# Grouped-query decode attention with a Mish MLP on one core: the first query weights in one load ahead of the first keys, two weight matrices in long rows with their operands turned on the chip, and the residual loaded mid-run

## The chip, the cores and the metric

One core of one Trainium2 chip. The metric is the device time of one execution in microseconds; the median of three runs of the kernel before is 1331.87 us (1331.69 to 1333.33).

## The reference

```python
# B=8 tokens, D=512, 32 query heads over 8 key/value heads, 8192 keys, head size 128, F=1792
xn = layernorm(x)                                    # no scale, no shift
q  = (xn @ wq) -> 8 x 32 heads x 128                 # wq [512, 4096]
s  = q . k_cache * 128**-0.5                         # 4 query heads share one key/value head
o  = softmax(s) . v_cache                            # k_cache, v_cache [8, 8, 8192, 128] fp32
A  = o @ wo                                          # wo [4096, 512]
h  = xn @ w1 + b1                                    # w1 [512, 1792]
m  = h * tanh(softplus(h)) @ w2                      # w2 [1792, 512]
out = x + A + m
```

All is fp32. Keys and values are 268 MB each, and the four weight matrices together 24 MB: nearly all of the work is reading 561 MB once.

## The kernel before

The work is cut into 32 units, `j = 8 * m + b`: one token `b` and one pair `m` of key/value heads (so 8 query heads). A unit needs one load of 8 MiB of keys and one of 8 MiB of values; each is one DMA that gives every partition one row of 64 KiB (`load_unit`, L127).

**Places.** One tile `kv` holds everything that streams: 160 KiB a partition. Values always land at `V_AT` (the first 64 KiB). Keys of even and odd units land at `K_AT[0]` and `K_AT[1]`, which start at 64 KiB and 96 KiB and overlap by half. Only the keys of unit 0 land at `V_AT`. So the values of unit 0 can be loaded only when the scores of unit 0 have read their keys to the end; the keys of unit j+1 when the first half of the scores of unit j is through; the values of unit j when `values(j-1)` has read the ones before. `w1` lands inside the place of the even keys (`W1_AT`), and the Mish layer computes there too, so the keys of unit 2 wait for the Mish layer. The four pieces of `wo` land at `V_AT` after the last unit, `w2` at `W2_AT`.

**Order.** The schedule is written by hand: every engine takes its instructions in the order of the code, and all large loads go through SP's one DMA queue in that order. A load is issued when SP reaches it and what occupies its place has been read.

**A unit** (the loop at L483): 32 score matmuls in two halves, with the load of the next keys issued between the halves (`scores`, L308); the row maximum on VectorE, turned over TensorE, and the exponential on ScalarE (`softmax`, L326); 32 matmuls of the unit before with its values, summed on VectorE (`values`, L374); then the issue of this unit's values; the masked query weights of the next unit (`key_weights`, L294, VectorE); the turning of the exponentials (`turn`, L352: 4 matmuls, 4 transposes and 2 long reductions on VectorE); and `merge` (L393), which puts the finished heads of the unit before into `oT`. In unit 0 the Mish layer (`mish`, L399) stands between. Once per pair of heads the query weights are loaded into `ws` (`load_q`), multiplied (`project`, L245) and spread over the partitions (`spread`, L277).

**The head of the program.** `x` comes over ACT's queue; VectorE normalizes it (L188 to L201) after it has built several selection matrices out of an identity that GpSimd makes. `wq` of the first pair is cut in two: 384 rows as three rows of 4 KiB per partition (`q0_3`, 1.5 MiB, SP's queue, ahead of the first keys), and the last 128 rows as 32 partitions with 16 KiB each (`q0_x`), in four DMAs that GpSimd issues, alternating with four DMAs for the bias `b1`. `q0_x` lies where the keys of unit 1 land. `project(0)` needs both parts, and two transposed copies of x for them (`xn3`, `xnx`).

**The tail.** After the last unit, `outputs` (L451) multiplies each of four pieces of `wo` with `oT`, `down` (L463) multiplies the three pieces of `w2` with the Mish result, and the residual, which was put into `xres` at the start by four matmuls (L225), is added (L550).

Of the kernel before, what the change touches and what calls it, by code (L numbers as in the profile page):

```python
# [53 lines left out]

D3 = 3
XQ = slice(64, 96)
XAT = ROW + ROW // 2


# [8 lines left out]
LOAD_Q, MAKE_Q, SPREAD_Q = 4, 5, 7  # L68


@with_exitstack
def kernel(
# [37 lines left out]
    gsel = const.tile([B, B, B], F32, name="gsel")  # L110
    xn4 = const.tile([P, CC, B], F32, name="xn4")
    xnT = const.tile([P, CC, B], F32, name="xnT")
    xn3 = const.tile([P, D3, B], F32, name="xn3")
    xnx = const.tile([P, CC, B], F32, name="xnx")
    qr = const.tile([P, DI, H2 * B], F32, name="qr")
    xres = const.tile([P, P], F32, name="xres")
    oT = const.tile([P, NP, H2, B], F32, name="oT")
# [24 lines left out]
    q0 = wq[:CC].rearrange("j p f -> (j p) f")  # L142
    q0_3 = ws[:, : D3 * BW]
    q0_x = kv[XQ, XAT : XAT + CC * BW]
    for r in range(4):
        n = FG // 8
        nc.gpsimd.dma_start(  # L147
            b1_sb[:, n * r : n * (r + 1)], b1.rearrange("(g c f) -> c g f", g=B, c=4)[r]
        )
        nc.gpsimd.dma_start(  # L150
            q0_x[r::4], q0[D3 * P :].rearrange("(e r i) f -> r e (i f)", r=4, i=CC)[r]
        )
    nc.sync.dma_start(q0_3, q0[: D3 * P].rearrange("(p i) f -> p (i f)", i=D3))
    k_t = {0: load_unit(kT, 0, V_AT)}
    w1_t = kv[:, W1_AT : W1_AT + 7168].rearrange("p (j f) -> p j f", j=2 * CC)
# [20 lines left out]
    for d in range(2):  # L176
        nc.vector.reduce_sum(
            rsel[:, d * REP : (d + 1) * REP],
            ident.rearrange("p (c d k h) -> p d h c k", c=2, d=2, h=REP)[:, d],
            axis=AX.XY,  # L180
        )
    nc.vector.tensor_copy(
        gsel, ident[:B, :B].rearrange("p (g o) -> p g o", o=1).to_broadcast([B, B, B])
# [20 lines left out]
    for c in range(CC):  # L204
        nc.tensor.transpose(
            M[:, 32 + c * B : 32 + (c + 1) * B], xc[:, c * P : (c + 1) * P], ident[:B, :B]
        )
    for c in range(D3):
        nc.tensor.transpose(
            M[:, 64 + c * B : 64 + (c + 1) * B], xc[:, c : D3 * P : D3], ident[:B, :B]  # L210
        )
    for c in range(CC):
        nc.tensor.matmul(
            M[XQ, 96 + c * B : 96 + (c + 1) * B],
            xc[:, D3 * P + c :: CC],
            ident[:B, :B],
            start=True,
            stop=True,
        )
    nc.vector.tensor_copy(xn3.rearrange("p c b -> p (c b)"), M[:, 64 : 64 + D3 * B])  # L220
    nc.vector.tensor_copy(xnx[XQ].rearrange("p c b -> p (c b)"), M[XQ, 96:128])
    nc.vector.tensor_copy(xn4.rearrange("p c b -> p (c b)"), M[:, 0:32])
    nc.vector.tensor_copy(xnT.rearrange("p c b -> p (c b)"), M[:, 32:64])
    for g in range(G):
        nc.tensor.matmul(  # L225
            M[Q * g : Q * g + B, 256:384],
            ident[:B, :B],
            x_sb[:, g * P : (g + 1) * P],
            start=True,
            stop=True,  # L230
        )
    nc.vector.tensor_copy(xres, M[:, 256:384])
# [12 lines left out]
    def project(m):  # L245

        w = ws.rearrange("p (c f) -> p c f", c=CC)
        terms = [(c, xn4[:, c, :], w[:, c]) for c in range(CC)]
        if m == 0:
            wx = q0_x.rearrange("p (c f) -> p c f", c=CC)  # L250
            terms = [(c, xn3[:, c, :], w[:, c]) for c in range(D3)]
            terms += [((c + D3) % CC, xnx[XQ, c, :], wx[:, c]) for c in range(CC)]
        for d in range(2):
            for n, (c, xt, wt) in enumerate(terms):
                nc.tensor.matmul(  # L255
                    H[Q * c : Q * c + B, :],
                    xt,
                    wt[:, d * 512 : (d + 1) * 512],
                    start=(n < CC),
                    stop=(n >= len(terms) - CC),  # L260
                )
# [12 lines left out]
        nc.vector.tensor_scalar_mul(qT, M[:, 192 : 192 + H2 * B], DH**-0.5)  # L274
        return qT
# [117 lines left out]
    def merge(j, os):  # L393
        m, b = divmod(j, B)
        nc.tensor.matmul(M[:, 168 : 168 + H2], os, hsel, start=True, stop=True)  # L395
        nc.vector.tensor_mul(oT[:, m, :, b], M[:, 168 : 168 + H2], RT.pop(j))


    def mish(w1_t, b1_sb, flat):  # L399
        hp = H[:, :FG]  # L400
        for c in range(CC):
            for g in range(G):
                nc.tensor.matmul(  # L403
                    hp[Q * g : Q * g + B, :],
                    xnT[:, c, :],
                    w1_t[:, c * 2 + g // 2, g % 2 * FG : (g % 2 + 1) * FG],
                    start=(c == 0),
                    stop=False,
                )
        for g in range(G):  # L410
            for e in range(2):
                nc.tensor.matmul(
                    hp[Q * g : Q * g + B, e * (FG // 2) : (e + 1) * (FG // 2)],
                    gsel[:, 2 * g + e, :],
                    b1_sb,
                    start=False,
                    stop=(e == 1),
                )
# [27 lines left out]
        nc.vector.tensor_copy(aT, turned.rearrange("p (j q) -> p j q", q=Q)[:, :, :B])  # L446
# [3 lines left out]

    def outputs(m, t):  # L451
        w = t.rearrange("p (u f) -> p u f", u=4)
        for d in range(2):
            for h in range(REP):
                nc.tensor.matmul(
                    A[Q * h : Q * h + B, :],
                    oT[:, m, d * REP + h, :],
                    w[:, d * 2 + h // 2, h % 2 * D : (h % 2 + 1) * D],
                    start=(m == 0 and d == 0),
                    stop=(m == NP - 1 and d == 1),  # L460
                )
# [14 lines left out]
    nc.sync.dma_start(w1_t, w1.rearrange("j p f -> p j f"))  # L476
# [3 lines left out]
    key_weights(0)  # L480

    v_t = {}
    for j in range(UNITS):  # L483
# [15 lines left out]
        if j + 1 < UNITS:  # L499
# [3 lines left out]
            key_weights(j + 1)  # L503
        if j == 0:
            mish(w1_t, b1_sb, kv[:, W1_AT : W1_AT + 6 * FG])
# [5 lines left out]
        if j > 0:  # L511
            merge(j - 1, os)
        if more and b == SPREAD_Q - 1:
# [20 lines left out]
    merge(UNITS - 1, os)  # L534
    outputs(NP - 1, w_o[NP - 1])
# [54 lines left out]
```

## Time and profile before

| | |
|---|---|
| median of 3 runs | 1331.87 us |
| the profiled execution, first to last instruction (its span) | 1330.5 us |
| DMA bytes | 561.79 MB, mean 422 GB/s |
| PE busy (matmul) | 984.8 us, 74% |
| VectorE busy | 516.0 us, 39% |
| ScalarE, GpSimd busy | 40.2 us, 6.4 us |
| share of the chain that ended last: DMA, PE | 73%, 22% |
| mean granted TensorE clock | 0.885 |

The page gives the profiled execution no time but its span; it is 1.4 us under the median of the runs. Times in the trace are microseconds from the first instruction. The rows used below are of six kinds: the page's 40 slices of the span (how busy the DMA engines were and what they moved), a table by stretches (`A:B`, then per engine its busy time and instructions in brackets, then the granted clock, the share of time in which the 16 DMA engines were busy, and GB/s), the chain of work that ended last (start, length, what), the timeline of one engine (start, length, engine, line, operation), who waited for whom, and the DMA issues with the median time to landing. "SPq" is the sequencer that issues SP's DMAs.

### The profile page before, as it was taken

What the parts mean: (1) busy time and instruction counts of PE and PEld (TensorE: products, weight loads), DVE (VectorE), ACT (ScalarE), POOL (GpSimd) and SP (SyncE); (2) the same over time, 40 slices, a digit from 0 to 9 for tenths busy, and PEclk for the clock granted to TensorE, in tenths of its full rate; (3) what the DMA queues carried; (4) which work ended last, traced back from release to release, by engine and by line L of the source; (5) the groups of instructions that cost most, each with busy time, mean ns of one, the idle gap of its engine ahead of it and who ended that gap; (6) DMA issues with size and microseconds to landing.
All of it is one profiled execution on the core that took longest, in us unless ns stands there. A gap on an engine that the chain in (4) does not pass through costs nothing.

```text
span 1330.5 us, 11234 instructions
## 1 busy us (share of the span) xinstructions
PE 984.8 (74%) x5071; PEld 338.3 (25%) x5071; DVE 516.0 (39%) x730; ACT 40.2 (3%) x88; POOL 6.4 (0%) x17
## 2 busy tenths in 40 slices
PE   1888776877867976776887777687786787677766
PEld 0422222222322222222322222222232222222222
DVE  2065444134443234444244444413444332444431
ACT  1000000000000000000000000000000000000000
POOL 1000000000000000000000000000000000000000
PEclk9999789988889888879988888998897998888898
DMA  9889999999999999999999999999999999999997
GB/s 341 338 346 432 420 438 436 436 428 436 428 436 434 434 432 428 427 439 438 426 432 432 438 430 434 426 438 434 430 430 434 432 434 436 428 428 434 430 415 321
DMA packets 13839, 561.79 MB, mean 422 GB/s; under 512 B 1464, under 2 KB 1592, under 8 KB 4800
## 3 DMA queue, kind: packets, MB, share of 16 engines
q1 hardware_dynamic: 13520, 560.53, 98.2%
q8 instruction: 39, 0.64, 0.2%
q0 software_dynamic: 256, 0.53, 0.1%
q10 hardware_dynamic: 16, 0.02, 0.0%
q14 instruction: 8, 0.07, 0.0%
HBM read 561.01 MB, written 0.07 MB: 422 GB/s over the span
## 4 chain that ended last, share of the span: by engine, by line
DMA 73%; PE 22%; DVE 2%; SPq 2%; issue 0%; POOL 0%; ACT 0%; DVEq 0%; POOLq 0%
DMA kv<-in_v 70%; PE o L378 19%; DMA kv<-in_wq 2%; DMA kv<-in_w 2%; SPq L528 2%; PE s L316 1%; DVE pt L366 1%; PE x L281 1%; PE h L255 0%; PE m L266 0%; PE h L403 0%; DVE kv L434 0%; DVE tr L360 0%; POOL kv L147 0%; DVE wk L299 0%
## 5 line engine op out<-in xcount | busy, mean ns | idle before, releaser
L316 PE MATMUL s<-kv,wk 128*64 128x512 f32 x2048 | 505.7, 657 | 180.7 <-DMA kv<-in_kT 178.1
L378 PE MATMUL o<-kv,pt 128*32 128x512 f32 x2048 | 262.3, 671 | 51.8 <-DMA kv<-in_v 42.2
L316 PEld LDWEIGHTS s<-kv,wk 128*64 128x64 f32 x2048 | 156.0, 152 | 505.0 <-issue 321.5
L366 DVE TENSOR_REDUCE pt<-tr 64x512 f32<-64x2048 f32 x64 | 241.3, 3771 | 1.6
L328 DVE TENSOR_REDUCE nm<-s 128x1 f32<-128x512 f32 x32 | 22.1, 692 | 374.2 <-PE s L316 374.1
L355 PE MATMUL x<-e,perm 128*128 128x512 f32 x256 | 126.4, 639 | 2.0 <-ACT qr L288 2.0
L378 PEld LDWEIGHTS o<-kv,pt 128*32 128x32 f32 x2048 | 68.4, 122 | 219.3 <-issue 164.9
L386 DVE TENSOR_SCALAR os<-o,isel 128x128 f32<-128x128 f32 x32 | 11.2, 351 | 265.4 <-PE o L378 265.4
L360 DVE STREAM_TRANSPOSE tr<-x 128x512 f32<-128x512 f32 x128 | 78.6, 671 | 0.0
L299 DVE TENSOR_TENSOR wk<-qr,mask 128x512 f32<-128x512 f32 x64 | 63.0, 1026 | 19.8 <-ACT qr L288 19.8
L355 PEld LDWEIGHTS x<-e,perm 128*128 128x128 f32 x256 | 48.9, 201 | 74.6 <-issue 72.2
L347 ACT ACTIVATE e<-s,nmx 128x512 f32<-128x512 f32 x32 | 22.0, 688 | 1092.8 <-DVE nmx L344 1092.8
L388 DVE SCALAR_TENSOR_TENSOR os<-o,isel,os 128x128 f32<-128x128 f32 x96 | 33.7, 351 | 3.4
L329 PE MATMUL m<-ident,nm 128*1 128x128 f32 x32 | 8.7, 273 | 30.1 <-DVE nm L328 30.1
L340 PE MATMUL m<-ident,nx 1*128 1x1 f32 x32 | 7.0, 219 | 24.2 <-DVE nx L336 24.2
L281 PE MATMUL x<-qT,tr 128*128 128x64 f32 x128 | 19.3, 315 | 3.0 <-ACT qr L288 2.7
L358 DVE RECIPROCAL rt<-m 128x8 f32<-128x8 f32 x32 | 6.6, 208 | 34.0 <-PE m L356 34.0
L281 PEld LDWEIGHTS x<-qT,tr 128*128 128x128 f32 x128 | 18.1, 226 | 6.2 <-ACT qr L288 3.3
L395 PE MATMUL m<-hsel,os 128*128 128x8 f32 x64 | 12.4, 266 | 9.3 <-DVE rt L358 9.3
L349 DVE TENSOR_SCALAR lsel<-rsel,l 128x8 f32<-128x8 f32 x32 | 7.4, 231 | 30.1 <-ACT e L347 30.1
L329 PEld LDWEIGHTS m<-ident,nm 128*1 128x1 f32 x32 | 2.5, 79 | 58.3 <-DVE nm L328 58.3
L356 PEld LDWEIGHTS m<-lsel,ones 128*128 128x128 f32 x64 | 12.2, 190 | 15.6 <-issue 15.3
(98 smaller groups left out, 172.2 us busy)
## 6 DMA issues: line engine op xcount, KB each, us to landing
kv<-in_wo SPq DMA_DIRECT2D x4, 2048.0 KB, 25.9
ws<-in_wq SPq DMA_DIRECT2D x3, 2048.0 KB, 35.2
kv<-in_w SPq DMA_DIRECT2D x1, 3584.0 KB, 24.7
kv<-in_w SPq DMA_DIRECT2D x1, 2048.0 KB, 37.0
ws<-in_wq SPq DMA_DIRECT2D x1, 1536.0 KB, 7.6
kv<-in_w SPq DMA_DIRECT2D x1, 1024.0 KB, 20.7
kv<-in_kT SPq DMA_DIRECT2D x32, 29.5
kv<-in_wq POOLq DMA_DIRECT2D x4, 128.0 KB, 25.1
```

Of the source, the lines that this page charges most:

```text
L281: nc.tensor.matmul(X[:, half, k * 64 : (k + 1) * 64], wide[:, half * 8 + k], qT, start=True, stop=True,)
L299: nc.vector.tensor_mul(w[:, :, d], q[:, :, d].to_broadcast([P, DI, NH * G, REP]), mask[:, d * NH * G : (d + 1) * NH * G] .rearrange("p (o ...
L316: nc.tensor.matmul(S[64 * c : 64 * (c + 1), :], w[:, i].rearrange("p d k h -> p (d k h)"), kk[:, i, c, :], start=(part == 0 and n == 0), s ...
L328: nc.vector.tensor_reduce(nm, S, axis=AX.X, op=ALU.max, negate=True)
L347: nc.scalar.activation(e, S, AF.Exp, bias=nmx, accum_out=l)
L355: nc.tensor.matmul(X[:, g], perm[:, g], e, start=True, stop=True)
L360: nc.vector.transpose(tr.rearrange("p (l t) c -> p t l c", t=TL)[:, tl], X.rearrange("p g (t q l) -> p t l g q", t=TL, q=PP)[:, tl],)
L366: nc.vector.tensor_reduce(pt8[half, :, :, d * REP : (d + 1) * REP].rearrange("p c y h -> p y c h"), tr[half].rearrange("p y (g c h) -> p y ...
L378: nc.tensor.matmul(O[Q * q : Q * (q + 1), :], pt8[:, c, TL * l : TL * (l + 1), :].rearrange("p t h -> p (t h)"), vt[:, 512 * n : 512 * (n ...
L388: nc.vector.scalar_tensor_tensor(os, O[:, DH * i : DH * (i + 1)], isel[:, i : i + 1], os, op0=ALU.mult, op1=ALU.add)
L395: nc.tensor.matmul(M[:, 168 : 168 + H2], os, hsel, start=True, stop=True)
L528: nc.sync.dma_start(t, w2_rows[:, lo * BW : hi * BW])
```

## The change

Five edits:

1. `wq` of the first pair is loaded whole, 2 MiB in rows of 16 KiB per partition, by the function that loads the other pairs, ahead of the first keys. The four GpSimd DMAs of `q0_x` go, and so do `xn3`, `xnx` and the extra terms of `project(0)`. `b1` goes to ACT's queue as one DMA behind `x`, so GpSimd issues no DMA any more.
2. `w1` is loaded as one row of 28 KiB per partition instead of eight rows of 3.5 KiB. Partition p then holds eight consecutive rows of half of `w1`; the normalized x is put into the matching order by two copies and eight transposes, and is masked by `fsel` into a half for either block of columns. `mish` therefore has 8 x 2 matmuls with 16 columns of x on two column groups, in place of 4 x 4 with 8 on four.
3. Each quarter of `wo` is loaded as one row of 16 KiB per partition instead of four of 4 KiB. For that `oT` is turned once per pair by a new function (`turn_outputs`), in units 9, 17, 25 and at the end.
4. The residual is not made at the start; seven small DMAs on ACT's queue load it in units 23 to 29 into `ws`, which is free by then.
5. Selection matrices `fsel`, `usel`, `vsel` are added, `gsel` moves into `kv`, and `aT` is filled by two copies instead of one.

```diff
-    for r in range(4):
-        n = FG // 8
-        nc.gpsimd.dma_start(b1_sb[:, n * r : n * (r + 1)], ...)
-        nc.gpsimd.dma_start(q0_x[r::4], ...)
-    nc.sync.dma_start(q0_3, q0[: D3 * P].rearrange("(p i) f -> p (i f)", i=D3))
+    nc.scalar.dma_start(b1_sb, b1.rearrange("(g f) -> g f", g=B))
+    load_q(0)
     k_t = {0: load_unit(kT, 0, V_AT)}
...
+    nc.vector.tensor_copy(xn4.rearrange("p c b -> p (c b)"), M[:, 0:32])
+    xd = kv[:B, W1_AT + 3 * D : W1_AT + 5 * D].rearrange("p (i k) -> p i k", i=W1R)
+    for h in range(2):
+        nc.vector.tensor_copy(xd...[:, h], xc.rearrange("p (c g i) -> p i c g", c=CC, i=W1R))
+    for i in range(W1R):
+        nc.tensor.transpose(M[:, 32 + i * B : 32 + (i + 1) * B], xd[:, i], ident[:B, :B])
+    for h in range(2):
+        nc.vector.tensor_scalar(xnT[:, :, h], M[:, 32 : 32 + W1R * B]..., fsel[:, h : h + 1], None, op0=ALU.mult)
...
-        if m == 0:
-            wx = q0_x.rearrange("p (c f) -> p c f", c=CC)
-            terms = [(c, xn3[:, c, :], w[:, c]) for c in range(D3)]
-            terms += [((c + D3) % CC, xnx[XQ, c, :], wx[:, c]) for c in range(CC)]
...
     def mish(w1_t, b1_sb, flat):
-        for c in range(CC):
-            for g in range(G):
-                nc.tensor.matmul(hp[Q * g : Q * g + B, :], xnT[:, c, :], w1_t[...], ...)
+        for i in range(W1R):
+            for n in range(2):
+                nc.tensor.matmul(hp[Q * n : Q * n + 2 * B, :], xnT[:, i]..., w1_t[:, i, n * FG : (n + 1) * FG], ...)
...
+    def turn_outputs(m):
+        half = 2 * REP * B
+        nc.tensor.transpose(M[:half, 256:384], oT[:, m % 2].rearrange("p h b -> p (h b)"), ident)
+        lm = work.tile([P, 512], F32, name="e").rearrange("p (i u q) -> p i u q", i=WOR, u=WOR)
+        nc.vector.tensor_mul(lm[:half], M[:half, 256:384]..., usel[:half]...)
+        for i in range(WOR):
+            nc.tensor.matmul(M[:, 384 + 2 * B * i : 384 + 2 * B * (i + 1)], lm[:half, i]..., vsel[:half]..., start=True, stop=True)
+        nc.vector.tensor_copy(oW[:, m]..., M[:, 384 : 384 + 2 * B * WOR])
...
+CUTS = ((0, 0, 1), (0, 1, B), (1, 0, 2), (1, 2, B), (2, 0, 3), (2, 3, B), (3, 0, B))
+    def residual(g, lo, hi):
+        nc.scalar.dma_start(xres[Q * g + lo : Q * g + hi, :], x[lo:hi, g * P : (g + 1) * P])
...
+        if 23 <= j < 23 + len(CUTS):
+            residual(*CUTS[j - 23])
...
+        if b == 1 and j > B:
+            turn_outputs(j // B - 1)
...
         nc.sync.dma_start(
-            w_o[m].rearrange("p (u f) -> p u f", u=4),
-            wo[4 * m : 4 * (m + 1)].rearrange("u p f -> p u f"),
+            w_o[m],
+            wo[4 * m : 4 * (m + 1)].rearrange("u p f -> (u p f)").rearrange("(p f) -> p f", p=P),
         )
...
     merge(UNITS - 1, os)
+    turn_outputs(NP - 1)
     outputs(NP - 1, w_o[NP - 1])
```

How the rows move, at the three places that the prediction speaks of. First the start of SP's queue, in the kernel before and then in the changed one; in brackets are the semaphores that an issue waits for (DMASW are DMAs that GpSimd issued, DMAHW those of SP and ACT).

```order
L153 DMA ws<-in_wq 128x3072
L131 DMA kv<-in_kT 128x16384
L476 DMA kv<-in_w 128x8x896 [waits DVE_49,DMAHW0_49,PE_49,Activation_49]
L131 DMA kv<-in_kT 128x16384 [waits DMASW5_49,DMASW3_49,DMASW7_49,DMASW1_49,PE_49]
L131 DMA kv<-in_v 128x16384 [waits DMAHW2_49,PE_49]
L131 DMA kv<-in_kT 128x16384 [waits DMASW4_49,DMASW6_49,DMASW2_49,DMAHW3_49,DMASW0_49,DMAHW4_49,DVE_49,PE_49]
```

```order
L126 DMA ws<-in_wq 128x4096
L132 DMA kv<-in_kT 128x16384
L501 DMA kv<-in_w 128x7168 [waits DVE_49,DMAHW0_49,PE_49,Activation_49]
L132 DMA kv<-in_kT 128x16384
L132 DMA kv<-in_v 128x16384 [waits DMAHW3_49,PE_49]
L132 DMA kv<-in_kT 128x16384 [waits DMAHW4_49,DMAHW2_49,DMAHW5_49,DVE_49,PE_49]
```

The keys of unit 1 (the fourth row) no longer wait for anything; before, they waited for the four `q0_x` DMAs and for the matmuls that read them. The values of unit 0 wait for the same things as before; the keys of unit 2 wait for one DMA of `b1` instead of four, and otherwise for the same.

Second the start of PE's queue, before and then changed, up to the first scores.

```order
L225 MATMUL m<-kv,ident 8x128 [waits DMAHW0_49,DVE_49]
L225 MATMUL m<-kv,ident 8x128 x3
L255 MATMUL h<-ws,xn_84 8x512 [waits DMAHW1_49]
L255 MATMUL h<-ws,xn_84 8x512 x2
L255 MATMUL h<-kv,xnx 8x512 [waits DMASW5_49,DMASW7_49,DMASW3_49,DMASW1_49]
L255 MATMUL h<-kv,xnx 8x512 x3
L266 MATMUL m<-bsel,e 128x8 [waits DVE_49,Activation_49]
```

```order
L210 MATMUL m<-ident,kv 128x8 [waits DVE_49,Pool_49]
L210 MATMUL m<-ident,kv 128x8 x3
L219 MATMUL m<-ident,kv 128x8 [waits DVE_49]
L219 MATMUL m<-ident,kv 128x8 x7
L248 MATMUL h<-ws,xn_81 8x512 [waits DMAHW1_49]
L248 MATMUL h<-ws,xn_81 8x512 x3
L259 MATMUL m<-bsel,e 128x8 [waits DVE_49,Activation_49]
```

The projection of the first pair (L255, now L248) waits for one DMA instead of five; ahead of it stand eight transposes (L219) that wait for a copy on VectorE.

Third PE's queue at the end of unit 9 in the changed kernel, where the first of three `turn_outputs` inside the loop stands (L451, L465); in the kernel before, the scores of unit 10 follow directly on the row of L388 (there L395).

```order
L371 MATMUL o<-kv,pt_90 32x512 x31
L348 MATMUL x_69<-e,perm 128x512 [waits Activation_49]
L348 MATMUL x_69<-e,perm 128x512 x3
L349 MATMUL m<-lsel,ones 128x8 [waits DVE_49]
L388 MATMUL m<-hsel,os 128x8 [waits DVE_49]
L451 MATMUL m<-ident,oT 64x128 [waits DVE_49]
L465 MATMUL m<-vsel,e 128x16 [waits DVE_49]
L465 MATMUL m<-vsel,e 128x16 x3
L309 MATMUL s<-kv,wk 64x512 [waits DMAHW0_49]
```

PE now waits twice for VectorE between the merge of one unit and the scores of the next, in three of the 32 units.

More of the change, by code (lines that the diff above doesn't have):

```diff
@@ L51 @@
 W2R = 7
-D3 = 3
-XQ = slice(64, 96)
-XAT = ROW + ROW // 2
+W1R = 2 * CC
+W1F = F // 2
+WOR = 4
 V_AT = 0
@@ L181 @@
         )
+    nc.vector.reduce_sum(
+        fsel, ident.rearrange("p (c h g) -> p h c g", h=2, g=2 * W1R), axis=AX.XY
+    )
+    nc.vector.reduce_sum(
+        usel[: P // 2],
+        ident[: P // 2, : P // 2].rearrange("p (u r) -> p u r", u=WOR),
+        axis=AX.X,
+    )
+    nc.vector.reduce_sum(
+        vsel[: P // 2],
+        ident[: P // 2, : P // 2].rearrange("p (u h b) -> p h b u", h=2, b=B),
+        axis=AX.X,
+    )
     nc.vector.tensor_copy(
-        gsel, ident[:B, :B].rearrange("p (g o) -> p g o", o=1).to_broadcast([B, B, B])
+        gsel,
+        ident[:B, :B]
+        .rearrange("p (h s o) -> p s h o", h=2, o=1)
+        .to_broadcast([B, G, 2, B]),
     )
@@ L473, in down @@
                 )
-    nc.sync.dma_start(w1_t, w1.rearrange("j p f -> p j f"))
+    nc.sync.dma_start(
+        kv[:, W1_AT : W1_AT + W1R * W1F],
+        w1.rearrange("j p f -> (j p f)").rearrange("(p f) -> p f", p=P),
+    )
     qT = project(0)
```

128 lines of the change are left out of this document (69 added, 59 removed).

## The prediction

> **What bounds the kernel now.** I read three views, coarse to fine. First the page's 40 slices (33 us each) and its chain:
>
> ```profile
> DMA  9889999999999999999999999999999999999997
> GB/s 341 338 346 432 420 438 436 436 428 436 428 436 434 434 432 428 427 439 438 426 432 432 438 430 434 426 438 434 430 430 434 432 434 436 428 428 434 430 415 321
> DMA 73%; PE 22%; DVE 2%; SPq 2%; issue 0%; POOL 0%; ACT 0%; DVEq 0%; POOLq 0%
> ```
>
> The DMA engines are busy in every slice, and from the fourth to the 38th they move about 433 GB/s: the stream is at its rate, and the PE part of the chain is only the link between one load and the next issue. Work taken off an engine in the middle buys nothing. But three slices at the head move 341 GB/s and the last two 415 and 321. So I ask the table by stretches where those bytes go missing (last two columns: share busy, GB/s):
>
> ```profile
> 0.00:90.00 90.00, 53.72 (x263) 23.93 (x265) 24.79 (x61) 8.47 (x13) 6.45 (x17) 1.00 0.85 332
> 90.00:130.00 40.00, 33.36 (x172) 10.86 (x168) 26.14 (x31) 0.78 (x2) 0.00 (x0) 0.91 0.98 420
> 130.00:1290.00 1160.00, 875.75 (x4388) 296.34 (x4388) 453.41 (x628) 30.39 (x72) 0.00 (x0) 0.88 1.00 433
> 5.00:35.00 30.00, 5.32 (x41) 2.23 (x41) 7.68 (x31) 2.21 (x4) 2.50 (x6) 1.00 1.00 362
> 45.00:62.00 17.00, 13.63 (x48) 8.84 (x50) 1.94 (x2) 1.17 (x2) 0.00 (x0) 1.00 0.99 429
> 62.00:73.00 11.00, 10.56 (x50) 3.23 (x46) 0.39 (x1) 0.00 (x0) 0.00 (x0) 1.00 0.02 6
> ```
>
> Two losses at the head. From 62 to 73 us nothing moves at all. From 5 to 35 us the engines are busy all the time, but at 362 GB/s. Who empties the queue at 62 us stands in the chain and in SP's waits of the first 80 us:
>
> ```profile
> 4.97 28.93 DMA kv<-in_wq
> 34.05 1.92 PE h L255 x8
> 38.50 3.68 PE h L255 x14
> 55.72 16.86 PE s L316 x64
> SPq L131 <- PE s L316: 30.0, 1, 30.0
> SPq L131 <- PE h L255: 8.2, 1, 8.2
> ```
>
> The last of GpSimd's four `wq` DMAs lands 28.93 us after its issue, at 33.9; only then does the projection run, and 21.7 us later (34.05 to 55.72) the first scores. SP stands 30.0 us before the load of the values of unit 0, until those scores end at 72.6, and stood 8.2 us before the keys of unit 1, whose place `q0_x` held until 42.2. Hence the hole.
>
> **The change, part by part.** The target is a stream without holes at 433 GB/s. In its first 90 us the kernel moves 90 x 332 = 29.9 MB; at 433 GB/s that takes 69.0 us, behind 1.8 us in which nothing has started yet: 19.2 us less. The 40 us after that at 420 GB/s hold 1.2 us more. This is the most there is at the head. Whether it is all had hangs on three issues.
>
> ```profile
> 1.26 0.65 POOL L147 DMA_DIRECT2D kv<-in_b  x1 [0.82 <-POOLq L577]
> 5.49 0.22 POOL masks.py:197 MEMSET ident<- 128x128 f32 x1
> 6.72 0.99 DVE L169 COPY perm<-ident 128x16 f32<-128x16 f32 x8 [4.23 <-POOL perm L160]
> 8.39 0.27 DVE L173 TENSOR_REDUCE isel<-ident 128x4 f32<-128x128 f32 x1
> 9.01 0.67 DVE L188 TENSOR_REDUCE st<-kv 8x1 f32<-8x512 f32 x1
> 14.19 0.61 PE L203 MATMUL m<-ident,kv 8*128 8x8 f32 x4 [14.19 <-DVE kv L201]
> 9.71 0.14 DVE L189 TENSOR_SCALAR st<-st 8x1 f32<-8x1 f32 x1
> 9.89 0.47 DVE L190 TENSOR_SCALAR kv<-kv,st 8x512 f32<-8x512 f32 x1
> ws<-in_wq SPq DMA_DIRECT2D x1, 1536.0 KB, 7.6
> ```
>
> *Scores of unit 0.* Without its eight DMAs (1.26 to 5.49) GpSimd makes the identity 4.2 us sooner, and VectorE loses its wait of 4.23 us; three more reductions (0.3 us each, by L173's row) cost 0.9 back. So the norm's chain starts at 5.7 instead of 9.01 and PE's first transposes run at 10.9 instead of 14.19. Then 0.6 us of transposes, 0.2 of copy, two new copies of 512 elements (0.5 each, by L190's row) and eight transposes (1.1, twice the row of four): the projection can start at 14.0. Its weights are there: three rows landed 7.6 us after the issue; a fourth is 1.2 us more, so 9.6. From the projection to the scores the old path takes 21.7 us; the second half has 8 instructions where it had 14 (3.68 us), 1.9 us as the row of 8 says, so 19.9. Scores from 33.9 to 50.8, in place of 72.6.
>
> *The queue meanwhile.* Behind 1.8 us: 2.1 MB of `wq`, 8.4 of keys, 3.7 of `w1`, 8.4 of keys, 22.5 MB, at 433 GB/s until 53.8. The values of unit 0 are issued at 50.8, three microseconds before the stream would run dry. No hole.
>
> *The next two issues* are tight, and here the change makes work longer.
>
> ```profile
> 74.53 3.19 PE L403 MATMUL h<-kv,xnT 128*8 128x448 f32 x32
> 90.50 0.22 DVE L446 COPY aT<-kv 128x112 f32<-128x112 f32 x1
> 72.60 0.33 SPq L131 DMA_DIRECT2D kv<-in_v  x1
> 90.79 0.33 SPq L131 DMA_DIRECT2D kv<-in_kT  x1
> 111.55 0.33 SPq L131 DMA_DIRECT2D kv<-in_v  x1
> ```
>
> The keys of unit 2 were issued 18.2 us after the end of the first scores, when the Mish layer was done. Its 32 instructions now run on two column groups, not four, so I take 6.3 us for 3.19, and 0.2 for the second copy: 21.5 us, at 72.3. The stream then has work until 53.8 + 19.4 = 73.2 (8.39 MB at 433 GB/s are 19.4 us). VectorE's turning of unit 0 shifts with it, so the values of unit 1 are issued 42.3 us after those scores instead of 38.95, at 93.1, where the stream ends at 92.6. Each issue needs about a microsecond before bytes flow. I put 1.0 us on the two, between 0 and 4 (the whole chain 3 us later). After that a unit has slack again: see below.
>
> *Rows of 16 and 28 KiB.*
>
> ```profile
> 1300.00:1310.00 10.00, 10.00 (x77) 2.43 (x73) 0.97 (x3) 0.00 (x0) 0.00 (x0) 0.80 1.03 409
> 1319.00:1327.00 8.00, 5.91 (x124) 3.04 (x120) 0.00 (x0) 0.59 (x1) 0.00 (x0) 0.87 0.49 203
> 1315.15 0.39 PE L395 MATMUL m<-hsel,os 128*128 128x8 f32 x2
> 1318.43 3.19 PE L455 MATMUL x<-kv,oT 128*8 128x512 f32 x16 [2.89 <-DMA kv<-in_wo]
> 1306.20 20.68 DMA kv<-in_w
> ```
>
> `wo` in 4 KiB rows moves at 409 GB/s, so 8.4 MB take 20.5 us. Rows of 64 KiB moved at 429 (45 to 62 us): 19.6. I take 0.9 us, between 0 and 1.1. `w1` is in the head's sum. The end is set by the last piece of `w2` (20.68 us after its issue), which comes that much sooner. What is late next would be PE: after the last merge (1315.15) stands the new turning, two matmul steps, a product and a copy, some 2.5 us, against a wait of 2.89 us for `wo` that covers it. The slow last 8 us (203 GB/s, half the engines empty) stay.
>
> The Trainium skill ("DMA: Bandwidth & Descriptors", Specifications) gives 512 B as the transfer from which line rate holds. By it 4 KiB rows have nothing to gain and the result would be 0.9 us higher; the trace, at 409 against 429 GB/s, disagrees, and I go by it.
>
> *Turning mid-run.* In units 9, 17 and 25 PE waits for VectorE before the next scores.
>
> ```profile
> 1248.34 20.24 SPq L131 DMA_DIRECT2D kv<-in_v  x2
> 1259.25 15.82 PE L316 MATMUL s<-kv,wk 128*64 128x512 f32 x64 [6.54 <-DMA kv<-in_kT]
> 1262.26 0.17 DVE L396 TENSOR_TENSOR oT<-m,rt 128x8 f32<-128x8 f32 x1
> 1278.59 7.07 PE L378 MATMUL o<-kv,pt 128*32 128x512 f32 x64 [1.48 <-DMA kv<-in_v]
> ```
>
> Here VectorE merges at 1262.4; a turning behind it would end at about 1264.4 and let the scores begin 5.2 us later than the 1259.25 at which their keys landed. The next key issue and the next value issue slip by as much. But the values were issued at 1248.3, eleven microseconds before the load ahead of them ended (1259.25), and the issue between the score halves comes some ten before 1278.6. The cover holds: nothing. If it were gone, it would cost up to 5 us three times.
>
> *Residual and bias.* Seven DMAs of 1 to 8 rows of 512 B go beside the stream, and `b1` as eight. The nearest rows are GpSimd's:
>
> ```profile
> q0 software_dynamic: 256, 0.53, 0.1%
> kv<-in_b POOLq DMA_DIRECT2D x4, 1.8 KB, 21.2
> ```
>
> Those 256 packets, 16 per engine, stood in the stretch of 5 to 35 us, which lost 30 x (1 - 362/433) = 4.9 us: 0.3 us for each packet an engine has to fit in. Two for each small row, one for the data and one for the semaphore, spread thinly: I take 0.5 us, between 0 and the rival's 5.
>
> **Sum.** 19.2 + 0.6 (half of the 1.2, since such slow spots may return) - 0.3 (a slower first microsecond of wq) - 1.0 + 0.9 - 0.5 = 18.9. From the profiled 1330.5 us that gives 1311.6; the median of the runs lies 1.4 us over that span, so **1313.0 us**. With its terms at their ends this case reaches from 1310 (19.2 + 1.2 + 1.1) to 1317 (19.2 - 0.3 - 4.0).
>
> **Rivals.**
>
> *The small packets pile up on one engine.* Every DMA engine carries the same bytes, so the end is when the slowest is done, and the last 8 us at 203 GB/s show that they do end apart. If one engine takes a packet of all seven residual DMAs, that is 14 x 0.3 = 4.3 us there, plus 0.6 for `b1`; if it is an engine that is already last, the end moves by 5: 1317.5 us. For it: nothing in the trace says which engines take them. Against: it must meet an engine already late. The Trainium skill (same page, "Why a DMA increments its semaphore by 16 and not by 1") says that a DMA of k rows runs on the k lowest-numbered engines; by it engine 0 does get all seven. No row here shows that, and which engines lag is not shown either.
>
> *The head is slow for another reason than GpSimd's packets*, say any stream in its first 40 us. The row that speaks for my reading is 45 to 62 us, 429 GB/s as soon as those DMAs are through; but 18 us may be too few. If the first 45 us stay at about 355, they lose 8 us again: 1320.5 us.
>
> *Slower than before.* A small transfer on ACT's queue is passed over as long as SP's queue is full, and the load that takes over its semaphore three units later is held until it lands. The row of `b1` above (1.8 KB, 21.2 us) shows small transfers landing late beside the stream. In the middle SP's queue is never empty, so each of the seven would first land when the stream runs dry. It decides from a loss of 2.7 us each (18.9 / 7); with a hole like the one at 62 us, say 6 us each, it gives 1313 + 42 = 1355 us. Against: those landed after 21 us, while the semaphore is next used three units, 116 us, later.
>
> *Nothing is gained*, because the middle was limited by PE after all and takes the lead back: 1332 us. Against: in the last fence PE waits 6.54 us for keys and 1.48 for values in one unit.
>
> **Numbers.** My case 0.75; the pile-up 0.12; the slow head 0.09; slower 0.02; nothing 0.02. A measurement of this kernel tells a difference of 0.2% (2.7 us) from none; all but the last two rivals lie far beyond it: faster 0.96, same 0.02, slower 0.02. The range of 8 in 10 takes my case and the two rivals next to it up to 1320; below, 1309, a microsecond under the sum of all upper ends.
>
> **What would show it.** In the changed profile: the first scores at 33 to 36 us and no stretch of the first 100 us with an idle DMA; 425 GB/s or more from 5 to 60 us; the values of unit 0 issued near 51, the keys of unit 2 near 72, the values of unit 1 near 93, and 19 us between the old and new landing of unit 1's values; `wo` at over 420 GB/s; from 130 us on the same 433. I am wrong if the head is gap-free and still slow, if a hole of more than 4 us opens at 73 or 93 us, or if the middle moves less than before.

## The result, and the profile after

The changed kernel takes **1313.38 us** (median of 4 runs, 1313.07 to 1313.74), the kernel before, run beside it, 1332.6 us. The ratio is 0.9859 with a 95% interval of 0.9845 to 0.9873: 19 us, or 1.4%, faster. The profiled execution took 1313.74 us with a span of 1312.0 us; the span before was 1330.5, so the spans differ by 18.5 us.

The page's slices and chain after:

```profile
DMA  9999999999999999999999999999999999999998
GB/s 404 442 418 433 430 440 424 441 430 436 431 432 434 418 430 436 430 434 428 436 434 430 404 442 422 442 428 432 442 422 440 426 438 422 442 430 432 430 423 337
DMA 66%; PE 28%; DVE 5%; issue 0%; ACT 0%; SPq 0%; DVEq 0%
```

The three slices at the head that moved 341, 338 and 346 GB/s move 404, 442 and 418 now. The rest looks as before, save that single slices (the 23rd, 404) have dipped. The table by stretches, with the columns as before:

```profile
0.00:90.00 90.00, 65.92 (x310) 27.91 (x314) 38.38 (x80) 9.25 (x15) 2.20 (x9) 0.96 0.99 425
90.00:130.00 40.00, 32.81 (x170) 11.32 (x162) 19.25 (x29) 0.78 (x2) 0.00 (x0) 0.91 0.99 420
130.00:1290.00 1160.00, 881.99 (x4386) 302.35 (x4389) 460.42 (x626) 29.57 (x70) 0.00 (x0) 0.86 1.00 431
5.00:35.00 30.00, 18.63 (x82) 13.03 (x84) 8.12 (x19) 4.55 (x8) 0.00 (x0) 1.00 1.02 439
45.00:62.00 17.00, 15.45 (x74) 5.05 (x70) 6.29 (x15) 2.64 (x4) 0.00 (x0) 1.00 1.03 444
92.00:99.00 7.00, 6.70 (x28) 2.92 (x28) 6.57 (x11) 0.00 (x0) 0.00 (x0) 1.00 0.93 346
424.00:436.00 12.00, 11.20 (x53) 3.38 (x49) 0.69 (x1) 0.00 (x0) 0.00 (x0) 1.00 0.98 404
741.00:753.00 12.00, 11.80 (x54) 3.51 (x50) 0.14 (x1) 0.00 (x0) 0.00 (x0) 0.98 0.96 389
1290.00:1300.00 10.00, 8.96 (x83) 2.97 (x75) 2.26 (x6) 0.00 (x0) 0.00 (x0) 1.00 1.00 425
```

The hole is gone and the stretch from 5 to 35 us went from 362 to 439 GB/s. New are three slow spots, 92 to 99 us (346 GB/s), 424 to 436 us (404) and 741 to 753 us (389). `wo` (1290 to 1300) moves at 425, against 409.

The chain shows where the 18.5 us lie. Pieces of it after, with start and length:

```profile
12.96 1.87 PE h L248 x8
32.76 16.71 PE s L309 x64
51.48 6.12 PE h L396 x32
82.90 8.64 PE o L371 x64
91.56 25.29 DMA kv<-in_v
```

The first scores begin at 32.76 instead of 55.72. The values of unit 1 are issued at 91.56 and land at 91.56 + 25.29 = 116.85. The same piece of the chain of before is

```profile
111.55 23.89 DMA kv<-in_v
```

which ends at 135.44: 18.6 us later. Twenty-nine units further on, PE takes up the values of unit 30 in PE's timeline after (before, in the prediction's row, at 1278.59):

```profile
1260.17 8.77 PE L371 MATMUL o<-kv,pt 128*32 128x512 f32 x64 [0.50 <-DMA kv<-in_v]
```

1278.59 - 1260.17 = 18.4. So the whole gain is there at 117 us. From the landing of unit 1's values to this row it takes 1143.2 us before and 1143.3 after: between 117 us and the end nothing is won or lost on balance, though three edits touch that part. (That the table reads 431 against 433 GB/s from 130 to 1290 us does not contradict this: in the changed kernel the last ten of these microseconds belong to `wo`. From 130 to 1260 us both kernels move 432.)

### The profile page after: what moved, and what is told of

The parts are those of the page before. It is cut to its first block, busy times and chain, and to the rows that moved or that the text cites. A ratio compares the mean times of both kernels' runs of the same rounds, so it can differ in the third digit from the quotient of the medians.

```text
span 1312.0 us, 11236 instructions
## 1 busy us (share of the span) xinstructions
PE 996.9 (76%) x5072; PEld 348.0 (27%) x5072; DVE 520.8 (40%) x742; ACT 40.2 (3%) x88; POOL 2.2 (0%) x9
## 2 busy tenths in 40 slices
DMA packets 11231, 561.80 MB, mean 428 GB/s; under 512 B 1280, under 2 KB 1448, under 8 KB 1584
## 4 chain that ended last, share of the span: by engine, by line
DMA 66%; PE 28%; DVE 5%; issue 0%; ACT 0%; SPq 0%; DVEq 0%
DMA kv<-in_v 63%; PE o L371 20%; PE s L309 5%; DMA kv<-in_w 3%; DVE pt L359 2%; PE x L348 1%; DVE tr L353 1%; PE x L274 1%; PE h L396 0%; PE m L465 0%; PE m L259 0%; PE h L248 0%; DVE nm L321 0%; DVE kv L427 0%; DVE e L455 0%
## 5 line engine op out<-in xcount | busy, mean ns | idle before, releaser
L371 PE MATMUL o<-kv,pt 128*32 128x512 f32 x2048 | 264.2, 675 | 51.9 <-DMA kv<-in_v 42.3
L348 PE MATMUL x<-e,perm 128*128 128x512 f32 x256 | 129.1, 651 | 2.0 <-ACT qr L281 2.0
L451 PE MATMUL m<-ident,oT 128*64 128x128 f32 x4 | 1.6, 392 | 29.6 <-DVE oT L389 29.6
L388 PE MATMUL m<-hsel,os 128*128 128x8 f32 x64 | 12.4, 267 | 9.3 <-DVE rt L351 9.3
```

Source lines behind the costliest of these rows:

```text
L348: nc.tensor.matmul(X[:, g], perm[:, g], e, start=True, stop=True)
L371: nc.tensor.matmul(O[Q * q : Q * (q + 1), :], pt8[:, c, TL * l : TL * (l + 1), :].rearrange("p t h -> p (t h)"), vt[:, 512 * n : 512 * (n ...
```

## Experiments

Two theories stood against each other for the head. Mine: the hole and GpSimd's packets are two separate losses, and edit 1 removes both. The rival: the first 40 us are slow for any stream. For the rest, my theory was a small gain from rows and nothing for the turning; the profile after made me doubt the second half of it. Kernels that ran side by side share the runs of the kernel before beside them (medians of the four sets 1331.98, 1332.53, 1331.80 and 1332.99 us). A span is that of the one profiled execution, a median that of all runs of a kernel.

### The head

**Edit 1 alone**, on the kernel before:

```diff
-    for r in range(4): ... nc.gpsimd.dma_start(b1_sb...); nc.gpsimd.dma_start(q0_x...)
-    nc.sync.dma_start(q0_3, ...)
+    nc.scalar.dma_start(b1_sb, b1.rearrange("(g f) -> g f", g=B))
+    load_q(0)
```

> The kernel before with the first edit alone (wq of the first pair in one load ahead of the keys, b1 on ACT's queue, no GpSimd DMA); w1, wo and the residual as before. If the head's order makes the gain: no idle stretch at 62 us, first scores near 33 us, the values of unit 1 landed by about 115 us instead of 135, span about 1311 us (116.4 us as in the changed kernel, minus 2.1 for the shorter Mish layer, plus 0.6 for w1 in short rows, plus 1.1 for wo in short rows). If the long rows carry a good part of it: 1318 us or more.

Measured: 1313.21 us (1313.08 to 1313.44), ratio 0.9857 (0.9842 to 0.9871), span 1311.6. A row of its table by stretches:

```profile
5.00:35.00 30.00, 20.07 (x90) 13.07 (x92) 6.50 (x16) 4.55 (x8) 0.00 (x0) 1.00 1.00 425
```

And its load of unit 1's values, in its chain:

```profile
87.20 28.44 DMA kv<-in_v
```

One edit of five gives the whole result; the other four together give nothing that these runs can tell. Its values of unit 1 land at 115.64, 1.2 us *before* those of the full change.

**Keys of unit 0 ahead of `wq`**, in the changed kernel:

```diff
-    load_q(0)
     k_t = {0: load_unit(kT, 0, V_AT)}
+    load_q(0)
```

> The changed kernel with the order of the first two loads exchanged: the keys of unit 0 ahead of the query weights. If the place of wq in the queue decides: wq lands near 27 us instead of 8, scores from about 47 us, the queue is empty from 54 to about 65 us, span 1323 to 1325 us. If it was only GpSimd's slow transfers that held the head: no hole worth 3 us, span about 1312 us.

Measured: 1327.83 us (1325.86 to 1329.7), ratio 0.9967 (0.9954 to 0.998), span 1324.1. A stretch of its table by stretches:

```profile
54.00:65.00 11.00, 10.20 (x49) 3.17 (x45) 0.69 (x1) 0.00 (x0) 0.00 (x0) 1.00 0.00 0
```

Three rows of its chain:

```profile
1.16 26.32 DMA ws<-in_wq
47.40 16.75 PE s L309 x64
106.27 22.93 DMA kv<-in_v
```

The same 2 MiB, issued one place later in the queue, land at 27.5 us; in the changed kernel they were there when the projection began, at 12.96. The scores shift by 14.6 us and a hole of 11 us, with not a byte in it, opens. The values of unit 1 land at 129.20, 12.4 us later than in the changed kernel, and the span is 12.1 us longer. But the profiled execution was the fastest of five, and the only one with a span in the expected 1323 to 1325 us; by the medians the exchange costs 14.5 us. So the hole's price, with GpSimd's packets out of play, is 12 to 14.5 us. What the other executions lost beyond the 12 is open.

**GpSimd's eight DMAs put back**, into unused space, with everything else as changed:

```diff
+    for r in range(4):
+        nc.gpsimd.dma_start(sb[:, n * r : n * (r + 1)], b1...[r])
+        nc.gpsimd.dma_start(sx[r::4], q0...[r])
     load_q(0)
```

> The changed kernel with the eight GpSimd DMAs of the kernel before added (same sizes, same 256 packets); what they load is not used, and only the keys of unit 1, which have time, wait for them. If 0.3 us per packet and engine is the price: 360 GB/s or so from 5 to 35 us, no hole, every landing after it 4.9 us later, span about 1317 us. If the head before was slow for another reason: the same 434 GB/s, span about 1312 us.

Measured: 1318.30 us (1316.61 to 1320.12), ratio 0.9894 (0.9877 to 0.9912), span 1316.8. Two stretches of its table:

```profile
5.00:35.00 30.00, 16.39 (x76) 12.26 (x76) 9.16 (x35) 4.13 (x8) 2.50 (x6) 1.00 1.01 384
35.00:60.00 25.00, 21.02 (x88) 6.45 (x90) 4.94 (x11) 2.48 (x4) 0.00 (x0) 1.00 1.02 437
```

Half a megabyte in 256 packets slows the stream from 439 to 384 GB/s while they are about, and no longer. The span grows by 4.8 us and there is no hole. A head that is slow by nature is ruled out: the same 30 us run at 439 without these packets.

That the packets alone cost the 4.8 us is not shown. GpSimd issues its eight DMAs before it fills the constants, so VectorE waits 4.23 us for GpSimd here too, PE's first transposes run at 14.67 instead of 9.99, and SP's issues come late all the way. The values of units 0 and 1:

```profile
54.08 0.33 SPq L132 DMA_DIRECT2D kv<-in_v  x1
96.13 0.33 SPq L132 DMA_DIRECT2D kv<-in_v  x1
```

In the changed kernel they leave at 49.48 and 91.56, 4.6 us sooner. The lower rate from 5 to 35 us loses 30 x (1 - 384/439) = 3.8 us, and the values of unit 1 land 4.0 us later (120.87 against 116.85). Either cause alone has the size of the loss, and no run had one without the other.

### The rows of `w1` and `wo`

**Edit 2 undone** (`w1` in eight rows of 3.5 KiB, the Mish matmuls on four column groups):

```diff
-                    hp[Q * n : Q * n + 2 * B, :], xnT[:, i]..., w1_t[:, i, n * FG : (n + 1) * FG],
+                    hp[Q * g : Q * g + B, :], xnT[:, c, :], w1_t[:, c * 2 + g // 2, ...],
...
-    nc.sync.dma_start(kv[:, W1_AT : W1_AT + W1R * W1F], w1..."(p f) -> p f")
+    nc.sync.dma_start(w1_t, w1.rearrange("j p f -> p j f"))
```

> The changed kernel with w1 again in 3.5 KiB rows and the Mish layer on four column groups (edit two undone). By the tight third issue: the Mish matmuls take 3.1 us instead of 6.1, the values of unit 1 are issued at about 88.5 us instead of 91.6, the slow spot at 92 to 98 us goes (2.1 us on the last engine), w1 costs 0.6 us more: span about 1310.5 us. If the rows are worth more than the handover: 1312.6 us or more.

Measured: 1313.56 us (1313.17 to 1314.44), ratio 0.986 (0.9845 to 0.9875), span 1311.4; from 90 to 130 us it moves more than the changed kernel (420):

```profile
90.00:130.00 40.00, 30.75 (x147) 10.01 (x145) 17.56 (x27) 0.78 (x2) 0.00 (x0) 0.87 0.99 428
```

Its values of unit 1 leave 4.8 us sooner (91.56 in the changed kernel):

```profile
86.79 0.33 SPq L131 DMA_DIRECT2D kv<-in_v  x1
```

The earlier issue is there, and the time is the same. Edit 2's longer rows and its longer Mish layer cancel as far as can be told; neither reading of the expectation is borne out alone.

**Edit 3 undone** (`wo` in rows of 4 KiB, no turning):

```diff
-        if b == 1 and j > B:
-            turn_outputs(j // B - 1)
...
-            wo[4 * m : 4 * (m + 1)]."u p f -> (u p f)"."(p f) -> p f"
+            wo[4 * m : 4 * (m + 1)]."u p f -> p u f"
```

> The changed kernel with wo again in 4 KiB rows and without the turning (edit three undone). Two things go opposite ways: the four pieces of wo take 20.4 us instead of 19.6 (plus 0.8), and the two gaps at 427 to 433 and 744 to 750 us, where the turning made an issue late, go. If those gaps only used up the lead of the faster DMA engines: span 1312.8 us. If they cost what the fast engines lost in them (2.1 and 3.2 us): about 1308 us.

Measured: 1314.27 us (1313.31 to 1314.58), ratio 0.986 (0.9843 to 0.9876), span 1312.3. Its median lies 0.9 us above the changed kernel's, but the two ranges overlap, and the ratios to the kernel before are the same (0.986 and 0.9859), so this is unclear. The first of the two stretches with a turning:

```profile
424.00:436.00 12.00, 9.32 (x66) 2.79 (x66) 1.71 (x7) 0.78 (x2) 0.00 (x0) 1.00 1.00 433
```

Without the turning the stream does not dip there (404 in the changed kernel), nor from 741 to 753 us (437 against 389), and the kernel is no faster for it. That the dips cost all that the fast engines lose in them, about 1308 us, is refuted.

### The residual's small DMAs

**Thirty-two DMAs of one row** in place of seven of one to eight rows:

```diff
-        if 23 <= j < 23 + len(CUTS):
-            residual(*CUTS[j - 23])
+        if 23 <= j < 31:
+            for n in range(4 * (j - 23), 4 * (j - 22)):
+                residual(n // B, n % B, n % B + 1)
```

> The changed kernel with the residual in 32 DMAs of one row each, four per unit in units 23 to 30, instead of seven. If one-row DMAs all go to one engine at 0.3 us for each of 2 packets: 64 x 0.3 = 19 us on that engine, less up to 4 us of lead, span 1325 to 1331 us, and the landings of all 16 engines spread by 15 us or more. If they are spread over the engines: 1.2 us each at the most, span 1312 to 1313 us.

Measured: 1314.57 us (1313.17 to 1316.61), ratio 0.9865 (0.985 to 0.9879), span 1311.4. Nothing piles up in the time. The profile counts 64 packets for these 32 DMAs, two for each. The Trainium skill ("DMA: Bandwidth & Descriptors", "Why a DMA increments its semaphore by 16 and not by 1") says that a DMA on this kind of queue runs on the lowest-numbered k engines, with k set by its shape. If one row is one engine by that rule, it would put all 64 packets on one engine, an estimated 19 us at 0.3 us each. The span agrees with no such price; which engines took them is not shown. One line of SP's waits is worth seeing:

```profile
SPq L132 <- DMA ws<-in_x: 24.7, 2, 17.1
```

Two of the bulk issues waited last for a small DMA, one of them for 17.1 us. This looks like my "slower" rival, but it is not a hold of 17.1 us. That load of keys (unit 25) left at 976.54, 17.4 us behind the values before it, and in the changed kernel the same load left 18.5 us behind its values (957.82 to 976.30). It had to wait for the first half of the scores of unit 24 in any case, which ended at about 975.7 (PE runs them from 968.75 to 982.70). What the small DMAs can have added there is under a microsecond. In the changed kernel, SP's waits name no residual DMA at all.

**The residual left out**, `xres` filled with zero:

```diff
-        if 23 <= j < 23 + len(CUTS):
-            residual(*CUTS[j - 23])
+        if j == 23:
+            nc.gpsimd.memset(xres, 0.0)
```

> The changed kernel without the seven residual DMAs; the residual is replaced by zeros, so the addition of x is left out of the result. Spread thinly: 0 to 0.5 us less, span 1311.5 to 1312.0 us. If they pile up on an engine that is last: 4 to 5 us less, 1307 to 1308 us.

Measured: 1315.62 us (1313.06 to 1315.92), ratio 0.9867 (0.9852 to 0.9882), span 1314.1, above both readings. Without these DMAs the kernel is not faster, so a pile-up of 4 to 5 us is not there. Its own scatter of 2.9 us is larger than the term of 0.5 us in question, so that term is not resolved.

### The turning mid-run

The trace after shows what I had not reckoned with. PE's timeline in unit 9:

```profile
415.53 0.42 PE L451 MATMUL m<-ident,oT 128*64 128x128 f32 x1 [9.78 <-DVE oT L389]
416.73 1.89 PE L465 MATMUL m<-vsel,e 64*128 64x16 f32 x8 [0.78 <-DVE e L455]
```

PE waits 9.78 us for `oT`, then turns, and the scores of unit 10, whose first half must be through before the next keys are issued, come late (418.55 us). SP's timeline there:

```profile
401.37 0.33 SPq L132 DMA_DIRECT2D kv<-in_v  x1
428.36 0.33 SPq L132 DMA_DIRECT2D kv<-in_kT  x1
```

The keys are issued 27.0 us behind the values, and 8.39 MB last 19.4 us. What the engines do just then (the table by stretches, share busy and GB/s last; rows this short are coarse):

```profile
426.00:428.00 2.00, 2.00 (x12) 0.70 (x10) 0.00 (x0) 0.00 (x0) 0.00 (x0) 1.00 0.76 328
428.00:429.00 1.00, 1.00 (x6) 0.28 (x4) 0.00 (x0) 0.00 (x0) 0.00 (x0) 1.00 0.31 131
```

The rate falls before the issue, while bytes still move. It looks as if some engines were idle and some still worked on the load ahead.

The third turning, in unit 25, waits as long (9.78 us), and its keys leave 26.6 us behind the values, but here the stream does not dip (437 GB/s from 1056 to 1068 us). In a repeat of the same kernel (below) it does (371). So the dips differ from one execution to the next.

To see what the turnings cost, I **moved the turnings one unit on, behind `values`**, where `oT` has long been merged:

```diff
             os = values(j - 1, v_t.pop(j - 1))
+        if b == 2 and j > B:
+            turn_outputs(j // B - 1)
...
-        if b == 1 and j > B:
-            turn_outputs(j // B - 1)
```

> The changed kernel with the three turnings inside the loop moved one unit later, to right after the values matmuls, where what they read is long ready and PE does not wait for VectorE's long reductions. The gaps at 427 and 744 us should go. If only the slowest DMA engine sets the end: the same span, 1312.0 us within 0.5. If the gaps cost: 1307 to 1309 us.

Measured: 1312.45 us (1312.12 to 1312.56), ratio 0.9847 (0.9832 to 0.9862), span 1310.8, between the two readings. The dips are gone:

```profile
424.00:436.00 12.00, 9.51 (x46) 2.60 (x46) 1.71 (x7) 0.78 (x2) 0.00 (x0) 0.80 1.01 437
```

Its next keys leave 6.1 us sooner than in the changed kernel (428.36):

```profile
422.29 0.33 SPq L132 DMA_DIRECT2D kv<-in_kT  x1
```

Here the scores of unit 10 begin at 412.74, when their keys have landed, so the turning had made them 5.8 us late (forecast: 5.2). The values ahead of the next keys, issued at the same time in both kernels (401.45 and 401.37), are taken up by PE here at 432.09, as soon as they have landed. If they land then in the changed kernel too, its late keys still left some four microseconds before the load ahead had landed, and the stream dipped all the same.

To tell whether the time follows, I ran **the changed kernel and this one again**, side by side.

> The changed kernel itself, unchanged, beside the next two on one chip: 1313.0 to 1313.8 us as before.

> The kernel with the turnings one unit later, again. If the late key issues behind the turnings do cost the last DMA engine something: 0.6 to 1.2 us under the changed kernel of this call. If the first comparison was chance between chips: the same within 0.3 us.

Measured: 1313.47 us (1312.84 to 1315.53; ratio 0.9866, 0.9847 to 0.9885) against 1313.12 us (1311.65 to 1314.27; ratio 0.9861, 0.9846 to 0.9876). A difference of 0.35 us between ranges of 2.7 is no finding.

**The Mish layer on four column groups as well**, with `w1` still in long rows:

```diff
-        for n in range(2):
-            nc.tensor.matmul(hp[Q * n : Q * n + 2 * B, :], xnT[:, i]..., w1_t[:, i, n * FG : (n + 1) * FG], ...)
+        for n in range(2):
+            for a in range(2):
+                q = 2 * n + a
+                nc.tensor.matmul(hp[Q * q : Q * q + 2 * B, :], xnT[:, i]..., wn[:, a], ...)   # 224 columns
```

> The turnings one unit later, and the Mish layer on four column groups of 224 columns instead of two of 448, with w1 still in 28 KiB rows: its matmuls should take 3.1 us instead of 6.1 and its VectorE chain about 7 us instead of 12, so the values of unit 1 are issued near 84 us instead of 91.6, the slow spot at 92 to 98 us goes and they have landed by 114.0 us instead of 116.4. If that is worth what the last engine lost there: 1.5 to 2 us under the kernel with the turnings alone, 1310.3 to 1311.0 us. If the lead of other engines covers it: the same as that kernel, 1312.4 us.

Measured, beside the last two: **1311.15 us** (1311.09 to 1311.33), ratio 0.9847 (0.9832 to 0.9862), span 1309.5. Two rows of its chain:

```profile
50.80 3.15 PE h L400 x64
85.91 29.02 DMA kv<-in_v
```

The stretch that was slow, in its table:

```profile
92.00:99.00 7.00, 3.38 (x10) 1.12 (x12) 6.95 (x3) 0.00 (x0) 0.00 (x0) 0.55 1.04 449
```

Twice the matmuls of half the width on twice the groups take 3.15 us instead of 6.12, on VectorE the chain works on 224 columns instead of 448, the values of unit 1 leave 5.7 us sooner (85.91) and land at 114.93, 1.9 us sooner than in the trace of the changed kernel. That trace was a late one, though: seven profiled executions with the same head take up these values between 115.1 and 116.9 us, 115.9 on average, and move 337 to 421 GB/s from 92 to 99 us; the two with a Mish layer on four groups and long rows take them up at 115.0 and 115.1. So the shorter Mish layer is worth about 0.8 us at this point. This was the fastest kernel of its set, its slowest run faster than every run of the other two. It is 2.0 us under the kernel with the turnings alone, as the first reading had it; the 2.3 us to the changed kernel are 0.18%, which is under what I called tellable.

**The same without moving the turnings** separates its two parts.

> The changed kernel with the Mish layer on four column groups and the turnings where the change has them (the kernel mish_four without the move of the turnings). It separates the two parts of mish_four. If the 2.0 us come from the head alone and the turnings cost nothing that tells in the time: values of unit 1 issued near 86, 92 to 99 us at over 430 GB/s, time 1311.0 to 1311.6 us as mish_four. If the turnings' waits cost what the faster DMA engines stand idle (404 and 389 GB/s in 424 to 436 and 741 to 753 us, about 0.8 to 1 us on the last engine): the head as above, but 1312.0 to 1312.8 us.

Measured: 1312.99 us (1312.34 to 1313.7), ratio 0.9852 (0.9835 to 0.9868), span 1311.9. The load in its chain, and the stretch with the turning:

```profile
86.26 28.81 DMA kv<-in_v
```

```profile
424.00:436.00 12.00, 11.00 (x52) 3.31 (x47) 0.85 (x3) 0.00 (x0) 0.00 (x0) 1.00 0.92 378
```

The head is that of the last kernel (landing at 115.07), the dip is back at 378 GB/s, and the time lies where it should if the dips cost 1 to 2 us. But the two kernels did not run side by side, the kernel before differed by 1.2 us between their sets, and their intervals overlap. The traces give one more measure, the time from PE's take-up of the values of unit 1 to that of unit 30. Six profiled executions without turnings in units 9, 17 and 25 take 1143.1 to 1144.8 us, 1143.7 on average; eight with them take 1143.3 to 1146.1, 1144.5 on average. That the dips exist and go away with the move is shown. That they cost about a microsecond is likely, and no more; in the profiled execution of the change itself (1143.3) they cost nothing that shows.

## Why the prediction held, and where it did not

The forecast was 1313.0 us, with its own case between 1310 and 1317; measured 1313.38. The mechanism, the order at the head, held; that the sum came within 0.4 us is partly luck, since terms that were off by a microsecond met.

*The norm's chain, the projection, the scores.* Forecast: first transposes at 10.9, projection at 14.0, scores at 33.9. Each came about a microsecond sooner (9.99, 12.96, 32.76), each step behind the other as worked out; the microsecond is there at the norm's first reduction (4.81, forecast 5.7). The row for PE's start:

```profile
9.99 0.61 PE L210 MATMUL m<-ident,kv 8*128 8x8 f32 x4 [9.99 <-DVE kv L208]
```

*The queue.* Values of unit 0 forecast at 50.8, measured 49.48; keys of unit 2 at 72.3, measured 70.54; values of unit 1 at 93.1, measured 91.56; the Mish matmuls at 6.3 us, measured 6.12. No hole, as said.

*The gain at the head.* 19.2 + 0.6 - 0.3 - 1.0 = 18.5 was forecast for it, 18.6 measured, and edit 1 alone gives it. At the landing of unit 1's values, the hole costs 12.4 us in its run and GpSimd's DMAs 4.0 in theirs; these make 16.4. The price of GpSimd's DMAs (4.8 us by the span, forecast 4.9) has the size of the forecast, but the forecast put it on the packets alone, and GpSimd's late constants, which it priced only in the chain to the scores, come with them in that run. What else was won, no run took alone. There was a second gap before, while the keys of unit 1 waited for `q0_x`; in the table of before:

```profile
40.00:44.00 4.00, 3.29 (x17) 1.27 (x14) 0.00 (x0) 0.59 (x1) 0.00 (x0) 1.00 0.89 316
44.00:46.00 2.00, 1.68 (x9) 1.59 (x8) 0.23 (x1) 0.00 (x0) 0.00 (x0) 1.00 0.08 33
```

Against 433 GB/s these six microseconds lack 4 x (1 - 316/433) + 2 x (1 - 33/433) = 2.9 us, and the new slow spot takes part of it back (next point). That leaves the sum near the 18.6, but executions with the same head differ by 1.8 us at this point, so the split is not closer than that.

*The two tight issues.* The term was 1.0 us, between 0 and 4. With a Mish layer on four column groups the spot at 92 to 99 us is gone and the values of unit 1 land about 0.8 us sooner than the average of the changed kernel's head, 1.9 sooner than in its own trace. So the term's size was right on average and half of it in the profiled execution. The head came out at the forecast there all the same: the values left 1.5 us sooner than forecast and landed 0.4 later, and that these met is luck.

*Rows.* For `wo`, 0.9 us is the upper end of what the runs show. Over the same 20 us (1280 to 1300), 4 KiB rows moved 415 GB/s in the run with edit 3 undone, and 16 KiB rows 426: 0.5 us for 8.4 MB. From PE's take-up of the values of unit 30 to the end, the three profiled executions with 4 KiB rows take 51.9 to 52.6 us, the eleven with 16 KiB rows 51.0 to 52.6, on average 52.3 against 51.5; in the pair of the change itself it is 51.9 against 51.8. No comparison of times settles it. For edit 2 the longer rows and the later issues come out even.

*The step that failed:* "The cover holds: nothing", for the turning mid-run. I took the cover as the time from an issue to the landing of the load ahead of it, some ten microseconds. By that measure it shrank but held in unit 9: 9.8 us with the turning moved, some four with the turning in its place, if the load ahead lands at the same time in both. The stream dipped all the same: 131 to 328 GB/s just before the issue at 428.36, 404, 389 and, in another run, 378 over twelve microseconds. This fits DMA engines that end apart: the first are done with the load ahead and wait for the next, while the last, which sets the landing, is still at work. Engine by engine that is not shown here, and so neither is why so little of it reached the end. My answer was nearly right for the time and wrong for the reason.

*Small packets.* 0.5 us was forecast; neither leaving them out nor making 32 of 7 moved the time beyond the scatter. The pile-up (1317.5) and the slow head (1320.5) are refuted; the rival "slower" has its price refuted, and its hold is not shown (under a microsecond at most, with 32 DMAs); "nothing is gained" fell with the result.

## What to carry to other kernels

In a kernel that streams, look for stretches where the DMA engines are idle or slow, and ask what the first issue behind each waits for: here a 2 MiB load moved one place forward in a queue was worth 12 us or more, and eight small DMAs from a second queue, with the late start that came with them, cost 5. Do not count the lead of an issue to the landing of the load ahead: here the stream slowed although, as far as can be told, some four microseconds of that lead were left. Four of the five edits together changed nothing that could be measured; before building one, set its whole possible gain (here at most 1 us for longer rows) against the scatter.

## What was not expected of the hardware

256 packets that GpSimd issued beside the stream came with 384 instead of 439 GB/s over 30 us, while 64 packets of 32 one-row DMAs on ACT's queue cost nothing that shows. Their number, size, queue and place all differ, so which of these makes the difference is not shown.

After the issue at 91.56, when 39.2 of the 39.3 MB issued before it had moved, the stream ran at 346 GB/s for 7 us although its engines show 93% busy. In the two kernels whose issue came over five microseconds sooner it ran at 449 and 431 in the same 7 us. Seven executions with the changed kernel's head moved 337 to 421 there, so the size differs from one execution to the next. Why the engines are busy and slow is not shown.
